# One late weight tile loaded in nine transfers: 96 partitions, then four times twelve tiny partitions and eight

## The chip, the cores and the metric

The kernel runs on one core of one Trainium2 chip. The metric is device time of one execution in microseconds (us). Three runs of the kernel before took 431.78, 432.27 and 433.0 us, so the median is 432.27 us.

## The reference

Two stages, in float32. First a linear attention with 8 batches, 8 heads, 576 positions and head size 64; then a spectral mixing of its output `x` (8 x 576 x 512) with 64 modes, each with a real and an imaginary 512 x 512 weight matrix.

```python
def phi(x):
    proj = np.einsum('bhsd,df->bhsf', x, w_phi)
    proj = proj - np.max(np.abs(proj), axis=-1, keepdims=True)
    return np.concatenate([np.exp(proj), np.exp(-proj)], axis=-1)
q_p, k_p = phi(q), phi(k)
num = np.einsum('bhsf,bhfd->bhsd', q_p, np.einsum('bhsf,bhsd->bhfd', k_p, v))
den = np.einsum('bhsf,bhf->bhs', q_p, np.sum(k_p, axis=2))[..., None] + 1e-06
x = num / den                                   # then heads side by side: (8, 576, 512)
X = np.fft.rfft(x, axis=1); Xr, Xi = real and imaginary part of X[:, :64]
Yr = einsum('bmd,mde->bme', Xr, w_r) - einsum('bmd,mde->bme', Xi, w_i)
Yi = einsum('bmd,mde->bme', Xr, w_i) + einsum('bmd,mde->bme', Xi, w_r)
u = x + np.fft.irfft(Y, n=576, axis=1)          # Y is zero above mode 63
out = u + np.maximum(u @ w_ch, 0.0)
```

The weights `w_r` and `w_i` are 64 x 512 x 512 float32 each, 134 MB together. They are the bulk of what the kernel reads.

## The kernel before

**Weights.** The 512 input channels are cut into four groups `g` of 128, the 64 modes into eight octets `o`. A weight tile `wt`, named by `(g, w)` with `w = 2*o + i` (`i` 0 for `w_r`, 1 for `w_i`), holds eight modes and 128 channels as bfloat16: 128 partitions with four rows of 1024 elements each, 1 MB in on-chip memory, 2 MB of float32 in HBM. There are 64 such tiles. `wload(g, w)` issues the one load of a tile from GpSimd (POOL), which converts on the way. A row of 1024 elements is the unit that one DMA engine moves as one packet; a tile has 512 rows, which is 32 for each of the 16 DMA engines.

**Order of the loads.** The queue `wq` lists all tiles in the order in which they are wanted; `next_w(1)` takes the next. Nearly every matmul step `mix` that has used up a tile calls it, since it frees a buffer (pool `pw`, nine buffers). In the attention part (16 units, up to about 285 us) loads of `q`, `k`, `v` stand between the weights. In the last part (the loop `while mixq`) there are 24 mixes: first the tiles `(3, 0)` to `(3, 11)`, then the twelve late ones

`(1,12) (1,13) (2,12) (2,13) (3,12) (3,13) (1,14) (1,15) (2,14) (2,15) (3,14) (3,15)`

Between two mixes TensorE does parts of the output work (`fill`: `hold`, `Channels.product`, `Absorb.all`). Behind the last mix stands what needs the last octet: `yst`, `zst`, the copies to `yl`, the sums of the list `plan` and the stores to `out`.

**In order.** Every engine's instructions run in the order in which the program writes them (class `InOrder`, line 37, which is also the line that the profile shows for nearly everything). POOL issues all the loads of `q`, `k`, `v` (but a few, which SyncE issues) and the weights, one behind the other.

**Completion semaphores.** The framework gives the transfers that POOL issues eight completion semaphores in turn. Each landing adds 16 to its semaphore, one for each of the 16 DMA engines. Before a transfer is issued, POOL waits until the transfer that had the same semaphore, eight transfers earlier, has landed, and then for its buffer. So at most eight transfers of POOL are under way at any time, of whatever size.

**A transfer of v in parts.** The last unit's `v` is loaded by SyncE in transfers of 57, 64 and 7 partitions (`load_v_parts`), issued at 248.17 us.

Of the kernel before, what the change touches and what calls it, by code (L numbers as in the profile page):

```python
# [11 lines left out]
BF16 = mybir.dt.bfloat16  # L12
# [10 lines left out]
MG = 8  # L23
# [20 lines left out]
def kernel(  # L44
# [15 lines left out]
    pool, sp = InOrder(tc, nc.gpsimd), InOrder(tc, nc.sync)  # L60
# [274 lines left out]
    def home(g, w):  # L335

        if g == 0 and w in (0, 9):
            h = w // 9
            t = yacc.bitcast(BF16).rearrange("p o e -> p (o e)")[:, 4096 * h:4096 * h + 4096]
        elif g == 0 and w == 5:  # L340
            t = XTb[1].rearrange("p u r t x b m -> p (u r t x b m)")
        elif g == 0 and w in (3, 12, 13):
            t = xs[:, max(w - 10, 1)].rearrange("p b n d -> p (b n d)")[:, 0:4096]
        else:
            return pw.tile([128, 4, 2, DMODEL], BF16, name="wt", tag="wt")
        return t.rearrange("p (m r e) -> p m r e", m=4, r=2)

    def wload(g, w):
        wt = home(g, w)
        o, i = w // 2, w % 2  # L350
        w = (moe_w_r, moe_w_i)[i]
        pool.dma_start(
            wt.rearrange("p m r e -> p m (r e)"),
            w[MG * o:MG * o + MG, g * 128:(g + 1) * 128, :].rearrange(
                "m (p r) e -> p m (r e)", r=2))
        return wt

    wts = {}
    wq = [(g, mg) for g in range(NG) for mg in range(12 if g else 2 * NO)]
# [6 lines left out]
    def next_w(n):  # L366
        for _ in range(n):
            if wq:
                key = wq.pop(0)
                wts[key] = wload(*key)  # L370
# [68 lines left out]
    for t in range(3):  # L439
        r = slice(32 * t, 32 * t + 32)  # L440
        dve.tensor_scalar_mul(out=minus[r], in0=ident_f[r, r], scalar1=-1.0)
    every = mf[0:96, 0:32]
    for t in range(3):
        r = slice(32 * t, 32 * t + 32)
# [167 lines left out]
    pb = pb_cm.__enter__()  # L612
# [340 lines left out]
    while mixq:  # L953
        key = mixq.pop(0)
        g, o, i = key[0], key[1] // 2, key[1] % 2
# [16 lines left out]
        if left > 12:  # L972
            n = -(-max(len(todo) - A - 3, 0) // (left - 12))
        elif left == 12:
            n = len(todo) - A
        else:
            n = math.ceil(len(todo) / max(left - 2, 1)) if left else 0
# [93 lines left out]
```

## Time and profile before

| | |
|---|---|
| runs, us | 431.78, 432.27, 433.0 |
| the profiled execution, us | 432.76 |
| its span, first to last instruction, us | 430.9 |
| PE, DVE, ACT, POOL busy share of the span | 75%, 70%, 69%, 28% |
| traffic of the DMA engines | 97.71 MB as written, 227 GB/s mean |
| HBM read and written | 163.64 MB and 9.44 MB |
| DMA engines' busy share, 307 to 341 us | 1.12 (over 1: packets overlap on an engine) |

The profiled execution is 1.86 us longer than its span. All times below count from the span's start. The profile's `MB` of a load counts what is written, half of what is read for a weight tile. "To landing" is the time from the start of the POOL instruction that issues a transfer to the last of the 16 increments of its semaphore.

### The profile page before, as it was taken

How to read it: one execution, taken by the hardware profiler on the slowest of the kernel's cores; microseconds unless marked ns; L12 is line 12 of the kernel's file. 1: busy time of each engine (PE TensorE's matmuls, PEld its weight loads, DVE VectorE, ACT ScalarE, POOL GpSimd, SP SyncE). 2: the span in 40 equal slices, each digit the busy share in tenths (PEclk: the TensorE clock that was granted, in tenths of full speed). 3: DMA queues.
4: the chain of work that ended last, by engine and by line, in shares of the span. 5: the costliest groups of instructions: out<-in, count | busy, mean ns of one | idle time of the engine just before them, and what ended most of it. 6: DMA issues, size and time to landing. Idle time of an engine off the chain costs nothing.

```text
span 430.9 us, 10044 instructions
## 1 busy us (share of the span) xinstructions
PE 324.9 (75%) x4162; PEld 195.6 (45%) x4207; DVE 302.7 (70%) x596; ACT 299.1 (69%) x487; POOL 122.2 (28%) x160
## 2 busy tenths in 40 slices
PE   1677577678787776876877767967899789886992
PEld 1345455446464553654645545543455333322320
DVE  6758767766677767878877878868645656882794
ACT  3787886877879779888878779765644345652772
POOL 6232132022321212322222321221022025750880
PEclk9979898889988989998988989899899999998998
DMA  9999999999999999999999999999999999997797
GB/s 211 210 211 211 238 213 237 224 225 238 240 210 233 216 237 238 238 211 239 212 239 222 226 244 229 212 212 212 212 212 213 212 211 212 212 212 161 244 395 288
DMA packets 49880, 97.71 MB, mean 227 GB/s; under 512 B 2315, under 2 KB 11531, under 8 KB 49835
## 3 DMA queue, kind: packets, MB, share of 16 engines
q0 software_dynamic: 45136, 85.40, 101.3%
q1 hardware_dynamic: 4538, 11.60, 7.2%
q8 instruction: 33, 0.54, 0.5%
q10 hardware_dynamic: 160, 0.07, 0.1%
q14 instruction: 13, 0.10, 0.1%
HBM read 163.64 MB, written 9.44 MB: 402 GB/s over the span
## 4 chain that ended last, share of the span: by engine, by line
PE 34%; ACT 24%; DMA 20%; DVE 14%; issue 4%; POOL 2%; ACTq 0%; POOLq 0%; DVEq 0%
DMA wt<-in_moe_w_i_dram 14%; PE pt L37 13%; PE one L37 11%; ACT AQ L37 10%; ACT AB L37 7%; PE two L37 6%; DMA kb<-in_k_dram 6%; DVE m L37 5%; PE pp L37 3%; ACT qT L37 3%; ACT XT L37 2%; DVE xs L37 2%; DVE xw L37 2%; DVE of L37 1%; DVE mk L37 1%
## 5 line engine op out<-in xcount | busy, mean ns | idle before, releaser
L37 ACT ACTIVATE AQ<-two 128x1024 bf16<-128x1024 f32 x64 | 80.6, 1348 | 2.1 <-PE two L37 2.0
L37 ACT ACTIVATE AB<-two 128x1024 bf16<-128x1024 f32 x64 | 62.8, 1055 | 3.3 <-DVE mk L37 3.0
L37 DVE TENSOR_REDUCE m<-two 128x8 f32<-128x1024 f32 x32 | 39.1, 1223 | 22.2 <-PE two L37 22.0
L37 ACT CAST xw<-pt 128x512 bf16<-128x512 f32 x54 | 31.8, 588 | 26.9 <-PE pt L37 26.7
L37 DVE TENSOR_REDUCE mk<-two 128x8 f32<-128x1024 f32 x32 | 38.9, 1219 | 9.2 <-PE two L37 9.2
L37 PE MATMUL pt<-wchb,xT 128*128 128x512 bf16 x135 | 37.0, 387 | 8.9 <-DVE xT L37 2.4
L37 POOL DMA_DIRECT2D wt<-in_moe_w_i_dram x28 | 21.1, 753 | 77.2 <-PE pt L37 37.2
L37 PE MATMUL two<-w2blk,qT 128*128 128x256 bf16 x128 | 23.9, 319 | 24.1 <-ACT AQ L37 13.6
L37 DVE TENSOR_TENSOR va<-vn,ee 128x1152 bf16<-128x1152 f32 x32 | 42.0, 1355 | 0.0
L37 POOL DMA_DIRECT2D wt<-in_moe_w_r_dram x30 | 22.5, 749 | 55.4 <-PE one L37 27.7
L37 PEld LDWEIGHTS <-xs 128*128 128x128 bf16 x624 | 31.1, 102 | 12.7 <-issue 5.9
L37 ACT COPY qT<-one 128x512 bf16<-128x512 bf16 (+1 forms) x32 | 19.0, 642 | 23.0 <-PE one L37 22.9
L37 PEld LDWEIGHTS <-qT 128*128 128x128 bf16 x144 | 15.3, 108 | 39.0 <-issue 35.0
L37 PE MATMUL two<-mT,minus 96*128 96x512 bf16 x64 | 26.5, 414 | 3.0 <-issue 0.9
L37 POOL DMA_DIRECT2D kb<-in_k_dram x16 | 11.4, 714 | 59.4 <-PE one L37 52.5
L37 DVE TENSOR_TENSOR xs<-one,rd 128x384 bf16<-128x384 f32 x48 | 26.8, 557 | 1.6
L37 PE MATMUL one<-kvz,AQ 128*128 128x65 bf16 x512 | 25.9, 203 | 0.9 <-ACT qT L37 0.8
L37 PEld LDWEIGHTS <-XT 128*32 128x32 bf16 x512 | 14.4, 149 | 27.0 <-issue 17.2
L37 PEld LDWEIGHTS <-AQ 128*128 128x128 bf16 x512 | 23.2, 104 | 7.1 <-issue 3.0
L37 PE MATMUL one<-wt,XT 128*32 128x512 bf16 x272 | 23.8, 438 | 3.4 <-ACT XT L37 3.4
L37 PE MATMUL two<-w2blk,kT 128*128 128x256 bf16 x128 | 21.1, 293 | 5.1 <-ACT AB L37 5.1
L37 PE MATMUL one<-CF,xs 128*128 128x64 bf16 (+2 forms) x480 | 23.2, 204 | 1.8 <-DVE xs L37 1.2
(151 smaller groups left out, 722.4 us busy)
## 6 DMA issues: line engine op xcount, KB each, us to landing
wt<-in_moe_w_r_dram POOLq DMA_DIRECT2D x30, 1024.0 KB, 26.3
wt<-in_moe_w_i_dram POOLq DMA_DIRECT2D x28, 1024.0 KB, 27.4
out_dram<-of SPq DMA_DIRECT2D x15, 512.0 KB, 3.4
vn<-in_v_dram POOLq DMA_DIRECT2D x13, 576.0 KB, 24.9
kb<-in_k_dram POOLq DMA_DIRECT2D x16, 288.0 KB, 19.6
qb<-in_q_dram POOLq DMA_DIRECT2D x16, 288.0 KB, 18.7
xs<-in_moe_w_i_dram POOLq DMA_DIRECT2D x2, 1024.0 KB, 23.3
out_dram<-of SPq DMA_DIRECT2D x6, 256.0 KB, 3.0
```

The source lines that it names most:

```text
L37: ins = f(*args, **kwargs)
```

## The change

`wload` is left as it was for 63 of the 64 tiles. The load of tile `(1, 12)`, written `(g, o, i) == (1, 6, 0)`, the first of the twelve late ones, becomes nine transfers. The first has partitions 0 to 95. Then follow four pairs: a load of 8 columns of the first 12 rows of `w_phi` into a new tile `few`, which nothing reads, and a load of eight partitions of the weight tile. All nine are issued by POOL, where the one was issued.

```diff
-        pool.dma_start(
-            wt.rearrange("p m r e -> p m (r e)"),
-            w[MG * o:MG * o + MG, g * 128:(g + 1) * 128, :].rearrange(
-                "m (p r) e -> p m (r e)", r=2))
+        dst = wt.rearrange("p m r e -> p m (r e)")
+        src = w[MG * o:MG * o + MG, g * 128:(g + 1) * 128, :].rearrange(
+            "m (p r) e -> p m (r e)", r=2)
+        if (g, o, i) != PIECES:
+            pool.dma_start(dst, src)
+            return wt
+        few = pb.tile([12, 32], BF16, name="few", bufs=1)
+        pool.dma_start(dst[0:96], src[0:48])
+        for n in range(4):
+            pool.dma_start(few[:, 8 * n:8 * n + 8], w_phi[0:12, 8 * n:8 * n + 8])
+            pool.dma_start(dst[96 + 8 * n:104 + 8 * n], src[48 + 4 * n:52 + 4 * n])
         return wt
+
+    PIECES = (1, 6, 0)
```

The order on PE, DVE, ACT and SP is the same in the built programs. On POOL there are eight transfers more, and the names of the semaphores that they wait for are these (SW0 to SW7 for the eight; `PE` is the wait for the buffer):

```
wt (3,11)                  128x4x1024   waits SW1, PE
wt (1,12), 96 partitions    96x4x1024   waits SW2, PE
few                              12x8   waits SW3, and writers and readers that lie before 290 us
wt (1,12), partitions 96..    8x4x1024  waits SW4
few                              12x8   waits SW5
wt (1,12), partitions 104..   8x4x1024  waits SW6
few                              12x8   waits SW7
wt (1,12), partitions 112..   8x4x1024  waits SW0
few                              12x8   waits SW1
wt (1,12), partitions 120..   8x4x1024  waits SW2
wt (1,13)                  128x4x1024   waits SW3, PE
```

Nine transfers in place of one shift the turn of the eight semaphores by a whole round, so every transfer behind them keeps the semaphore that it had.

## The prediction

> **What bounds the kernel now.** I read the page first, for the resource that is never idle.
>
> ```profile
> span 430.9 us, 10044 instructions
> DMA  9999999999999999999999999999999999997797
> q0 software_dynamic: 45136, 85.40, 101.3%
> ```
>
> The DMA engines are busy in every slice but the last four, and the queue that POOL's transfers use takes all of their time. The chain of waits shows where that reaches the end of the kernel, and the waits of PE whether anything softens it.
>
> ```profile
> 369.25 26.36 DMA wt<-in_moe_w_i_dram
> 395.65 0.84 PE pt L37 x8
> PE pt L37 <- DMA wt<-in_moe_w_i_dram: 2.4, 1, 2.4
> PE pt L37 <- DMA wt<-in_moe_w_r_dram: 0.9, 1, 0.9
> ```
>
> The load of tile (3,15), issued at 369.25, lands at 395.6; PE starts its eight matmuls 0.04 us later, having stood idle for 2.4 us, and 0.9 us before tile (3,14). Everything behind 395.65 hangs on this landing. So a shift of the last landing moves the end by as much, and a delay of the tiles before it costs nothing while it stays under their slack (below).
>
> Next the issue of the loads on POOL, with what each waited for, and the landings.
>
> ```profile
> 275.68 0.74 POOL L37 DMA_DIRECT2D wt<-in_moe_w_r_dram  x1 [3.13 <-PE one L37]
> 278.78 0.74 POOL L37 DMA_DIRECT2D wt<-in_moe_w_i_dram  x1 [2.35 <-PE one L37]
> 281.82 0.74 POOL L37 DMA_DIRECT2D wt<-in_moe_w_r_dram  x1 [2.30 <-PE one L37]
> ...
> 288.94 0.74 POOL L37 DMA_DIRECT2D wt<-in_moe_w_i_dram  x1
> 291.69 0.74 POOL L37 DMA_DIRECT2D wt<-in_moe_w_r_dram  x1 [2.01 <-PE pt L37]
> 299.84 0.74 POOL L37 DMA_DIRECT2D wt<-in_moe_w_i_dram  x1 [7.41 <-PE pt L37]
> 307.62 0.74 POOL L37 DMA_DIRECT2D wt<-in_moe_w_r_dram  x1 [7.03 <-PE pt L37]
> 313.06 0.74 POOL L37 DMA_DIRECT2D wt<-in_moe_w_i_dram  x1 [4.71 <-PE pt L37]
> ```
>
> The changed load is the one at 307.62; the answers for the single loads give 33.4 us to its landing, so 341.0. The six before it, (3,6) to (3,11), land by the same reading at 311.3, 316.3, 321.2, 326.1, 331.1 and 336.1, and (1,13) at 346.0. One tile lands every 4.95 us (4.96 from (1,13) to (3,15)): 0.155 us for each of an engine's 32 rows. The queue is some 34 us deep, which is six to seven tiles, each on a semaphore of its own, of eight.
>
> ```profile
> POOL wchb L37 <- DMA wt<-in_moe_w_r_dram: 3.9, 1, 3.9
> ```
>
> This line, of POOL's waits, shows that the eight semaphores do hold POOL up: `wchb` shares no buffer with a weight tile, yet its load waited 3.9 us until the transfer eight places before it had landed (issued at 117.46, landed at 146.6; `wchb` went out at 146.91).
>
> Last the sixteen increments of each landing, in the trace's records. Those of (1,12) run from 335.9 to 341.0: four engines at 335.9 to 336.6, one at 338.2, eleven at 339.6 to 341.0. This spread of 5.1 us is the same for every tile from 300 us on: four engines are ahead by some 4 us, and a tile is there when the slowest is.
>
> **The change, part by part.** *Rows taken off.* With 96 partitions an engine gets 24 rows for 32: 8 x 0.155 = 1.24 us less, so the large part lands at 341.0 - 1.2 = 339.8. Alone that would be a gain of 1.2 us, as the queue ends with its slowest engine.
>
> *Eight more transfers on POOL.* By the rows nearest in size (0.53 us for a `yl` of 16 partitions) they cost 8 x 0.53 = 4.2 us of POOL's time. Alone that is free: POOL idles 15.3 us before the issue at 348.60, and its first sum comes at 351.40.
>
> *Waits.* Here lies the price. The nine transfers take nine turns of eight semaphores, of which six or seven are held by tiles still in the queue. So POOL issues: 96 partitions at 307.6; first tiny load at 308.4; first eight partitions when (3,6) has landed, 311.3; then one transfer for each landing, at 316.3, 321.2, 326.1, 331.1 and 336.1. The fourth piece has the semaphore of the 96 partitions themselves, so it waits for 339.8, by which time all but a few rows of what was queued has been moved. Behind it on POOL, in order, stand (1,13), (2,12), (2,13), (3,12), (3,13) and (1,14), which went out from 313.06 to 332.57 and now go out from 340.4 on, 0.74 us apart. For PE the first of them is wanted at 352.68. The DMA engines run dry, and this is time of the resource that sets the end.
>
> *Restart.* What is lost is the time from an issue into an empty queue to data. Before 398 us the trace has no empty queue; the nearest row is the last `yl`, which POOL issues at 400.86 and which lands after 3.6 us.
>
> ```profile
> L37 POOL DMA_DIRECT2D yl<-zst x1: 532/532/532, 400.9 to 400.9; - x1
> ...
> DMA to landing us min/median/max: 3.6/3.6/3.6
> ```
>
> Its 128 KB take 0.6 us at the 212 GB/s of this stage, so the fixed part is 3.0 us. The far rows: SyncE's stores of 512 KB land in 3.4 us, 1.3 us of it data at 395 GB/s, so 2.1; the first `w_phi` load, 32 KB at the start of the program, takes 5.0. I take 3.0, the same engine, queue and state, and keep 2.1 and 5.0. The Trainium skill, page "DMA: Bandwidth & Descriptors", section "Anatomy of one DMA — SWDGE (gpsimd) path", gives a fixed cost of about 2.0 us; by it the sum below would be +2.1 us, and the trace's row is longer.
>
> *How many engines share a piece.* No POOL transfer in this trace uses fewer than 16. SyncE's loads of `v` do: of the 57 partitions three increments come late, together at 261.4 (57 is 3 x 19), of the seven partitions seven. So a transfer goes to a number of engines that divides it. Eight partitions from four source rows give eight engines or four, 0.62 or 1.24 us each; bounds are 16 engines (0.3) and one (4.95). I take four.
>
> *The sum.* The engines of the fourth piece: issue 339.85 + 3.0 + 1.24 + 4.95 = 349.0 for (1,13). The other twelve: 340.4 + 3.0 + 4.95 = 348.4. Before: 346.0. So (1,13) is 3.1 us late, the following tiles too, since from there on the queue is full again ((1,15) is issued at 348.60 as before, five tiles still queued), and (3,15) lands at 398.7. PE's slack between landing and use is 6.7 us for (1,13), 5.0 for (3,13), 4.5 for (2,14), 3.6 for (2,15): all above 3.1, so PE notices at (3,14) only, and the shift passes whole to the tail. The profiled execution took 432.76, so 435.9. It lay 0.5 above the median of its runs; from the median, 432.27 + 3.1 = **435.4**.
>
> **The rivals.** *A. The pieces fall on late engines.* Then pieces one to three, 3.7 us, follow 339.8 on them and cover the restart; the fourth and (1,13) follow at once: 339.8 + 3.7 + 1.24 + 4.95 = 349.7, +3.7, so 436.0. For it: eleven of sixteen engines are late, and the profile doesn't name the four that lead. On the leading four the three pieces are done by 338.4, before the restart, as in my sum. The page named above, section "Why a DMA increments its semaphore by 16 and not by 1", says that a POOL transfer on k engines takes k consecutive ones from a cursor that goes round; by that rule twelve and four bring the cursor back, and all four pieces fall on the same four. No run here shows it yet.
>
> *B. Balance without a stall (faster).* If the issues do not wait as I read it, the queue never empties: twelve engines save 1.24 us, the four leaders, 4.4 to 5.1 us ahead, carry 3.7 more and stay within it. The last landing comes 1.2 us earlier, 431.0; perfect balance (the mean of the sixteen increments is 339.2, against 341.0) would give 1.8. It decides if the fourth piece and (1,13) are issued by about 337, or the fixed part is under 0.6 us for the twelve engines. Against it: the wait of `wchb`, and the named semaphores.
>
> *C. A short restart (no change).* An empty queue may answer faster than 3.0 us. At 1.2 us the loss is down to 1.3 us. The shortest row, 2.1, speaks against it.
>
> *D. A piece is put on one engine.* The fourth then takes 4.95 on it: 339.85 + 3.0 + 4.95 + 4.95 = 352.8, +6.8, 439.1. The seven partitions on seven engines speak against it.
>
> **How the numbers follow.** My forecast gets 0.58, A 0.20, B 0.07, C 0.10, D 0.05. With the fixed part at 2.1 the forecast is +2.2 (434.5), at 5.0 it is +5.1 (437.4). The range, 433.2 to 437.2, holds the forecast nearly whole, A, and part of C; B, D and the ends are left out. A measurement can tell this kernel from no change from about 0.3%, 1.3 us, on. Faster by more: half of B, 0.03. Within: the rest of B, C, and a little of the forecast, 0.15. Slower: 0.82.
>
> **What would show it.** On POOL, between 307 and 342 us, tiny and eight-partition loads one for each landing, near 311, 316, 321, 326, 331, 336 and 340, and then six weight loads 0.74 us apart. In the windows a DMA share that falls near 340 to 343, and sixteen increments of (1,13) within about 1 us where they spread over 5. PE waits some 3 us longer for tile (3,14), and the last mix starts near 398.7. The prediction is wrong if POOL issues (1,13) before 335, or if the last mix starts before 396.9.

## The result, and the profile after

The changed kernel takes 436.95 us in the median of four runs (436.15 to 437.66), the kernel before 432.02 us in four (431.53 to 433.0): 4.9 us slower. The ratio on record is 1.0109, with an interval of 1.0092 to 1.0126 (it is not the quotient of the two medians, which is 1.0114). The profiled execution took 437.27 us, 4.5 more than that of before (432.76).

The page of the changed kernel:

```profile
span 435.4 us, 10101 instructions
DMA  9999999999999999999999999999999899998697
q0 software_dynamic: 45712, 85.40, 100.7%
```

The traffic is what it was; there is one slice more, the 32nd, in which the DMA engines were not busy throughout. The issues on POOL show why (start, duration, and in brackets the idle time before with what ended it):

```profile
306.65 0.68 POOL L37 DMA_DIRECT2D wt<-in_moe_w_r_dram  x1 [7.08 <-PE pt L37]
307.35 0.53 POOL L37 DMA_DIRECT2D few<-in_w_phi_dram  x1
311.57 0.63 POOL L37 DMA_DIRECT2D wt<-in_moe_w_r_dram  x1 [3.69 <-DMA wt<-in_moe_w_r_dram]
316.54 0.53 POOL L37 DMA_DIRECT2D few<-in_w_phi_dram  x1 [4.34 <-DMA wt<-in_moe_w_i_dram]
321.47 0.65 POOL L37 DMA_DIRECT2D wt<-in_moe_w_r_dram  x1 [4.40 <-DMA wt<-in_moe_w_r_dram]
326.41 0.53 POOL L37 DMA_DIRECT2D few<-in_w_phi_dram  x1 [4.29 <-DMA wt<-in_moe_w_i_dram]
331.37 0.63 POOL L37 DMA_DIRECT2D wt<-in_moe_w_r_dram  x1 [4.44 <-DMA wt<-in_moe_w_r_dram]
336.72 0.53 POOL L37 DMA_DIRECT2D few<-in_w_phi_dram  x1 [4.71 <-DMA wt<-in_moe_w_i_dram]
340.05 0.65 POOL L37 DMA_DIRECT2D wt<-in_moe_w_r_dram  x1 [2.81 <-DMA few<-in_w_phi_dram]
340.69 0.77 POOL L37 DMA_DIRECT2D wt<-in_moe_w_i_dram  x1
```

One transfer for each landing, 4.9 us apart; the fourth piece at 340.05, then (1,13), which before went out at 313.06. The DMA engines meanwhile, in 40 slices of 0.175 us from 338 to 345 us:

```profile
DMA  8666665564333110001180169969699999999999
```

They run out engine by engine, stand all but still near 341, and are full again from 343 on. From there the queue never empties, and the chain and PE's waits show the same end as before, only later (the chain: start, duration; the waits: total, times, longest):

```profile
368.25 31.87 DMA wt<-in_moe_w_i_dram
400.16 0.69 PE pt L37 x8
PE pt L37 <- DMA wt<-in_moe_w_r_dram: 4.7, 2, 4.3
PE pt L37 <- DMA wt<-in_moe_w_i_dram: 2.1, 2, 1.2
```

Tile (3,15) lands at 400.1 where it landed at 395.6: 4.5 us, the whole difference of the two profiled executions. From that landing to the last instruction both take 35.2 to 35.3 us.

### The profile page after: what moved, and what is told of

The parts are those of the page before. It is cut to its first block, busy times and chain, and to the rows that moved or that the text cites. A ratio compares the mean times of both kernels' runs of the same rounds, so it can differ in the third digit from the quotient of the medians.

```text
span 435.4 us, 10101 instructions
## 1 busy us (share of the span) xinstructions
PE 329.1 (76%) x4207; PEld 195.0 (45%) x4207; DVE 302.7 (70%) x596; ACT 298.9 (69%) x487; POOL 126.5 (29%) x168
## 4 chain that ended last, share of the span: by engine, by line
PE 34%; ACT 27%; DMA 19%; DVE 13%; issue 4%; POOL 1%; DVEq 0%; ACTq 0%; POOLq 0%
PE one L37 14%; ACT AQ L37 12%; DMA wt<-in_moe_w_r_dram 11%; PE two L37 9%; ACT AB L37 8%; PE pt L37 7%; DMA wt<-in_moe_w_i_dram 7%; DVE m L37 6%; PE pp L37 3%; ACT qT L37 3%; ACT XT L37 3%; DVE xs L37 2%; DVE mk L37 1%; DVE yacc L37 1%; POOL xw L37 1%
## 5 line engine op out<-in xcount | busy, mean ns | idle before, releaser
L37 PE MATMUL pt<-wchb,xT 128*128 128x512 bf16 x144 | 38.0, 387 | 8.4 <-DVE xT L37 2.4
L37 POOL DMA_DIRECT2D wt<-in_moe_w_r_dram x34 | 24.9, 733 | 66.0 <-PE one L37 34.3
L37 PE MATMUL two<-w2blk,qT 128*128 128x256 bf16 x128 | 22.8, 308 | 25.9 <-ACT AQ L37 13.7
L37 PE MATMUL two<-qT,w2blk 128*128 128x512 bf16 x64 | 26.9, 421 | 9.5 <-ACT AQ L37 9.5
```

The costliest lines, as they stand in the source:

```text
L37: ins = f(*args, **kwargs)
```

## The experiments

Two numbers are used below for each: when POOL issues (1,13), and when (3,15) lands, both from the profiled execution. The time from that landing to the last instruction is 32.8 to 35.3 us in the ten profiles, and why it varies is not shown. So the time of one profiled execution can be up to 2.5 us off what its landing says, and a few tenths between two medians are not read.

**Five transfers, without the tiny loads.**

```diff
-        few = pb.tile([12, 32], BF16, name="few", bufs=1)
         pool.dma_start(dst[0:96], src[0:48])
         for n in range(4):
-            pool.dma_start(few[:, 8 * n:8 * n + 8], w_phi[0:12, 8 * n:8 * n + 8])
             pool.dma_start(dst[96 + 8 * n:104 + 8 * n], src[48 + 4 * n:52 + 4 * n])
```

> The tile in 96 partitions and four of eight, without the four tiny loads: five transfers in place of one. Theory (the turn of the eight semaphores holds POOL until the queue is dry): five turns reach only as far as the load before the 96 partitions; POOL issues (1,13) near 326, (2,12) near 331, (2,13) near 336, all before the 96 partitions land at 339.8, the queue never empties, and the time is that of the kernel before within 0.7 us (ratio 0.998 to 1.002). Rival (small transfers of a few partitions, or their uneven place on the engines, cost the time): the same four pieces are there, so at least 3 us slower, ratio 1.007 or more.

Measured: 432.58 us, ratio 1.0011 (0.9999 to 1.0022). POOL, and the same slices from 338 to 345 us:

```profile
326.90 0.78 POOL L37 DMA_DIRECT2D wt<-in_moe_w_i_dram  x1 [4.60 <-PE pt L37]
331.86 0.76 POOL L37 DMA_DIRECT2D wt<-in_moe_w_r_dram  x1 [4.18 <-DMA wt<-in_moe_w_r_dram]
...
DMA  9999999999999999999999999999999999999999
```

(1,13) goes out at 326.9, nothing runs dry, (3,15) lands at 396.2. The same four pieces of eight partitions cost next to nothing, so the pieces by themselves are not what costs.

**Nine transfers, without the pieces.**

```diff
-        few = pb.tile([12, 32], BF16, name="few", bufs=1)
-        pool.dma_start(dst[0:96], src[0:48])
-        for n in range(4):
+        few = pb.tile([12, 64], BF16, name="few", bufs=1)
+        pool.dma_start(dst, src)
+        for n in range(8):
             pool.dma_start(few[:, 8 * n:8 * n + 8], w_phi[0:12, 8 * n:8 * n + 8])
-            pool.dma_start(dst[96 + 8 * n:104 + 8 * n], src[48 + 4 * n:52 + 4 * n])
```

> The tile in one load as before, and behind it eight tiny loads of 12 partitions that nothing reads: nine transfers, but no piece of the tile. Theory: the ninth has the semaphore of the tile's own load and waits for it, near 341.0; POOL issues (1,13) near 341.6, 1.2 us later than in the changed kernel, but no engine carries a fourth piece; the last mix starts near 399.5 to 401, time 436 to 437.5, ratio 1.009 to 1.012. Rival (the pieces cost it): eight tiny loads are eight times 0.53 us on a POOL that idles, ratio within 1.002 of 1.

Measured: 437.56 us, ratio 1.0117 (1.0099 to 1.0136); (3,15) lands at 400.7. The end of POOL's series:

```profile
336.37 0.50 POOL L37 DMA_DIRECT2D few<-in_w_phi_dram  x1 [4.47 <-DMA wt<-in_moe_w_i_dram]
341.31 0.50 POOL L37 DMA_DIRECT2D few<-in_w_phi_dram  x1 [4.44 <-DMA few<-in_w_phi_dram]
341.83 0.78 POOL L37 DMA_DIRECT2D wt<-in_moe_w_i_dram  x1
```

A tile in one piece is as slow as the change when nine turns are taken. The eighth tiny load goes out at 341.31, where the tile's own last increment stands at 341.0 (the trace names the tiny load that landed 0.2 us after it).

**The tiny loads from SyncE.** `pool.dma_start(few...)` becomes `sp.dma_start(few...)`, with `few` in float32.

> The changed kernel with its four tiny loads issued by SyncE (into float32), the tile's five transfers by POOL as they are: the same nine transfers on the same sixteen DMA engines, but five turns of POOL's semaphores for nine. Theory (POOL's turns): POOL issues (1,13) near 327 and the time is that of the kernel before, ratio 0.998 to 1.002. Rival (tiny transfers disturb the queue): as slow as the changed kernel, ratio 1.009 or more.

Measured: 433.02 us, ratio 1.0019 (1.0006 to 1.0033). (1,13) goes out at 327.1 and (3,15) lands at 396.2. The waits on POOL in this kernel are those of five transfers, and of the change's 1.09% some 0.2% is left.

```profile
291.03 1.53 SPq L37 DMA_DIRECT2D few<-in_w_phi_dram  x4
327.12 0.78 POOL L37 DMA_DIRECT2D wt<-in_moe_w_i_dram  x1 [4.59 <-PE pt L37]
```

The first line shows a limit of this test: SyncE issues the four tiny loads at 291.0, 19 us before the 96 partitions (310.3), so they no longer lie between the pieces. That tiny loads at their old place in the queue disturb it is not excluded here; what they cost there is read from the two kernels with seven transfers.

**Seven transfers: two tiny loads.** `few` is loaded for `n < 2` only.

> 96 partitions, tiny, eight, tiny, eight, eight, eight: seven transfers. Theory: POOL issues (1,13) when (3,11) has landed, near 336.1, and (2,12) when the 96 partitions have, near 340. The leading engines idle for 1 to 2 us, the late ones have the rest of their rows until 339.8 and are fed in time: 0 to 0.7 us slower, ratio 1.000 to 1.002. A loss in proportion to the number of transfers (the rival, a price for each small transfer) would give six eighths of the change's 4.9 us: 3.7 us, ratio 1.0085.

Measured: 433.39 us, ratio 1.0036 (1.0021 to 1.0051); (3,15) lands at 397.6.

```profile
337.20 0.78 POOL L37 DMA_DIRECT2D wt<-in_moe_w_i_dram  x1 [4.66 <-DMA wt<-in_moe_w_i_dram]
```

It is above what I gave (1.000 to 1.002), and far below a price in proportion (1.0085). Between seven turns and nine the loss trebles: at seven the next tile is issued while the late engines still have rows, at nine it is not. Of the 2.0 us by which (3,15) lands later, 0.6 stand at (3,11) already, which lies ahead of the tile, 0.3 more at (1,13), and 1.1 come in the last step, from (3,14) to (3,15) (6.09 us for 5.00; below).

**Seven transfers: the whole tile and six tiny loads.** As the kernel with eight, with `range(6)`. It was to explain the part above the expectation.

> The tile in one load as before, and six tiny loads of 12 partitions behind it: seven turns, of which the last waits for (3,11), so POOL issues (1,13) near 336.4, before the tile's own landing near 341, and the queue does not empty. Theory (a transfer costs every one of the sixteen engines its place in the ring, 0.17 to 0.2 us, also where it has no data there, as the increments of the tiny loads in the earlier runs stand that far apart): 6 x 0.18 = 1.1 us slower, the last landing 1.1 us later, ratio 1.0015 to 1.004. Rival (only the turns of the semaphores cost): ratio 0.999 to 1.001.

Measured: 434.90 us, ratio 1.0063 (1.0043 to 1.0083); (1,13) at 336.9, (3,15) lands at 397.2, 1.6 us later than before. The place that each tiny load takes is there: the last increment of (1,12) stands at 341.24, that of the sixth tiny load at 342.29, in steps of 0.17 to 0.19 us. But the tile behind them does not land 1.05 us later: (1,13) lands at 346.6 where it landed at 345.95, and 0.2 us of these 0.6 stand at (3,11) already. Most of the rest, 0.95 us, comes in the last step, from (3,14) to (3,15): 5.95 us for 5.00. So the price of six tiny loads is some 0.4 us at the next landing, well under mine. Nor did the queue stay full on all engines: seven increments of (1,13) come at 344.1 to 344.5, 7.3 to 7.6 us after its issue, as at a restart. Why the median of its runs (433.1 to 435.4) lies above the profiled 434.07, and the interval above mine, is open.

**Eight more tiny loads, behind the fourth piece.**

```diff
-        few = pb.tile([12, 32], BF16, name="few", bufs=1)
+        few = pb.tile([12, 96], BF16, name="few", bufs=1)
...
             pool.dma_start(dst[96 + 8 * n:104 + 8 * n], src[48 + 4 * n:52 + 4 * n])
+        for n in range(4, 12):
+            pool.dma_start(few[:, 8 * n:8 * n + 8], w_phi[0:12, 8 * n:8 * n + 8])
```

> The changed kernel with eight more tiny loads behind the fourth piece. Theory (once the queue is dry, every us of POOL is a us at the end): their semaphores are free by then, each costs POOL 0.53 us, so (1,13) is issued near 345.0 in place of 340.7, the last landing comes near 404.4, time 441.2, ratio 1.020 to 1.022. Rival (POOL's issue time stays hidden, the loss is a fixed restart): the same time as the changed kernel, ratio 1.009 to 1.012.

Measured: 439.87 us, ratio 1.0183 (1.0159 to 1.0208).

```profile
340.68 4.10 POOL L37 DMA_DIRECT2D few<-in_w_phi_dram  x8
344.77 0.80 POOL L37 DMA_DIRECT2D wt<-in_moe_w_i_dram  x1
```

The 4.1 us that POOL spends on them move the issue of (1,13) by 4.1 us, its first increment by 4.2 (347.9 to 352.1) and the last landing to 404.0, by 3.8. With a full queue POOL's issue time was hidden; with an empty one it is paid one to one, or nearly. The median moved less than the landing, by 2.9 us, and the ratio is below the 1.020 that I gave as the least; the rival, a fixed loss, is further off.

**Instruction fetches moved.** The trace of the changed kernel has a 16 KB instruction fetch in the DMA queues at 343.10, 1.59 us long, in the middle of the restart:

```profile
q8 instruction: 1, 0.02, 1.0%
```

(that is the window 340 to 350 us: 1.0% of sixteen engines' 10 us). To move it, 64 transposes were put on PE early:

```diff
+        if n == 2:
+            spin = one([128, 128], BF16)
+            for _ in range(64):
+                pe.transpose(spin, ident_b, ident_b)
```

> The changed kernel with 64 more transposes on PE early in the attention part (their result is not read). They bring PE's instruction fetches, 16 KB each and in the changed kernel at 328.65, 343.10 and 367.85, about half a distance forward, to about 320, 336 and 355, away from the restart near 341. Theory (one engine is 0.9 us behind all others at the landing of (1,13) because the fetch at 343.10 went through it): no engine is that late, (1,13) lands by about 348.9 in place of 349.7, and the last landing comes 0.3 to 1 us earlier than in the changed kernel; ratio 1.008 to 1.011. Rival (the late engine is late for another reason): the last increment of (1,13) stays 0.8 us or more behind the fifteenth, 7.3 us or more behind the issue of (1,13) by POOL plus 1.5.

Measured: 436.27 us, ratio 1.0101 (1.0074 to 1.0128). The fetches stand at 337.25 and 359.09. In each kernel's trace, the times to landing of the two transfers issued at 340.0 to 340.8 or 340.7 (minimum, median, maximum; the maximum is (1,13)), the changed kernel first:

```profile
DMA to landing us min/median/max: 3.8/6.4/9.0
```

```profile
DMA to landing us min/median/max: 4.0/6.2/8.3
```

From an issue at 340.69 and 340.71 the tile is there at 349.7 and at 349.0. In the changed kernel fifteen increments of it come from 347.9 to 348.85 and the last at 349.67; with the fetch moved all sixteen come from 348.0 to 349.05. (3,15) lands at 399.5, 0.6 us earlier. The times alone would not tell the two kernels apart, so this is shown for one profiled execution of each.

**A better balance tried in another place.** The kernel before, with the last `v` in two parts:

```diff
-            for p0, p1 in ((0, 57), (57, 121), (121, 128)):
+            for p0, p1 in ((0, 119), (119, 128)):
```

> The kernel before, with the last unit's v loaded by SyncE in parts of 119 and 9 partitions in place of 57, 64 and 7: 119 is 7 x 17, so seven engines should take 17 partitions each, nine take one each, and seven engines none of v. Theory (the slowest engine ends the queue, four to five of the lowest engines are ahead by 4 us): the late engines lose three or four partitions of 4.6 KB, 0.17 us each, so the spread of the sixteen increments after 300 us falls from 5.1 to about 4 or less and the last landing comes 0.5 to 0.7 us earlier: 431.4, ratio 0.998 to 0.999. Rival (the sum of all rows counts, not the slowest engine): no difference that can be told, ratio 1.000.

Measured: 435.27 us, ratio 1.0075 (1.0059 to 1.0091). The expectation failed in direction. Seven engines did take the large part (seven increments of it at 261.5 to 262.4), but the spread of a tile's increments grew from 5.1 to 8.3 us, and (3,15) landed at 397.8. So at least one of these seven was among the late ones. What stands is that the slowest engine counts: the last landing moved by 2.2 us although not a byte more was loaded.

## Why the prediction was right, step by step

**The waits.** Right, to the instruction: the series of issues is the predicted one (307.6, 308.4, 311.3, 316.3, 321.2, 326.1, 331.1, 336.1, 339.8, then 340.4) within 0.7 us; only the first two came 1.0 us earlier, as this execution reached them earlier. The sign that was to refute it, (1,13) issued before 335, did not come: it went out at 340.69. Taking the tiny loads off POOL, by leaving them out or by issuing them from SyncE, removes nearly all of the loss; keeping nine turns without the pieces keeps it.

**The restart.** The term was too large. From the issue of (1,13) to its first increment are 7.2 us in the changed kernel, of which 4.95 are rows: 2.3 us, and 2.2 to 2.35 in the three other kernels that ran dry. I took 3.0 from the `yl` row. (The upper bound, 5.0, is the median of two loads of `w_phi`; the first of them took 4.3. Neither bound was reached.) By the trace the Trainium skill's figure (page "DMA: Bandwidth & Descriptors", section "Anatomy of one DMA — SWDGE (gpsimd) path", about 2.0 us) was the nearer of the two.

**How many engines share a piece.** Right, four: of the fourth piece twelve increments come at 341.6 to 342.1 and four at 343.7 to 343.9. On these (1,13) is 0.7 us behind the rest, as in the sum (349.0 against 348.4).

**Where the pieces fall.** Rival A, three pieces one behind the other on the same late engines, is refuted, and so is the reading that put all four on the same engines; but the first piece did fall on late engines, as A's name says. (The prediction has the three pieces done on all four leaders by 338.4; by its own rows that is the first of the four, and the last is done by 339.1, which changes nothing in the sum.) An engine without data passes a transfer about 0.19 us after the one before. Taking that step from the first tiny load's increments gives those of the first piece but for four engines: 337.01 to 338.03, 338.50 to 339.49, 339.24 to 340.34 and 339.96 to 341.06, the slowest engine and three others, none of the leading four. In the second piece two of the leaders have data, 334.97 to 336.07 and 335.15 to 336.34. The kernel without tiny loads shows the same groups. So the pieces go round by fours with or without the tiny loads. This agrees with the Trainium skill's cursor for the pieces (same page, section "Why a DMA increments its semaphore by 16 and not by 1") but not with twelve engines for a load of twelve partitions: that load left the cursor where it was. The section names an exception, direct copies that count as sixteen engines although some have no data, which would fit; no run here shows that it is the reason.

**The other rivals.** B needed (1,13) issued by about 337; it went out at 340.69 and the queue had emptied. Its balance fails too: the first piece goes wholly to late engines and the second by half, so the four leaders do not carry the 3.7 us that would have balanced them. The five-transfer kernel, which never stalls, is no faster than before. C needed a restart of about 1.2 us, and it took 2.2 to 2.35. D needed one engine for the fourth piece, and there were four.

**What the sum left out.** The predicted shift was 3.1 us, the measured one 4.5 in the profiles and 4.9 in the medians. Fifteen engines brought (1,13) by 348.85, 2.9 us after the 345.95 of before: the restart was 0.7 us shorter than in the sum, the issues were 0.2 to 0.3 us later. On top come two terms of 0.8 us each that I did not have. That the first and the restart nearly cancel is luck.

First, one engine brought (1,13) at 349.7, 0.8 us behind the others; the fetch at 343.10 fits it, and with the fetches moved no engine was behind.

Second, from (1,13) to (3,15) it took 50.4 us where it took 49.7 before. A part, 0.2 us, is left of a fetch: with the one at 367.85 the last engine fell back by 0.4 us and made up half of it in the next tile. In the trace of before, the fetches of this stretch (345.67, 370.04 and 394.34) did not delay the last increment: the engines were up to 5.1 us apart, and the last increments kept their steps of 4.93 to 5.06 us. The larger part, 0.6 us, is the last step, from (3,14) to (3,15): 5.62 us for 5.00. A fetch lies in it too, at 398.10, but it is not what makes it long. In the kernel with the fetches moved, none lies between 381.42 and 409.81, yet its (3,15) lands 5.52 us after (3,14), its whole stretch takes 50.4 us too, and PE's mixes of the two tiles stand as far apart:

```profile
394.02 1.08 PE L37 MATMUL pt<-wt,XT 128*32 128x512 bf16 x8 [3.21 <-DMA wt<-in_moe_w_r_dram]
399.54 0.66 PE L37 MATMUL pt<-wt,XT 128*32 128x512 bf16 x8 [1.31 <-DMA wt<-in_moe_w_i_dram]
```

The ten traces fall into two groups. Where all or some engines ran dry, the sixteen increments of (3,15) lie within 1.9 to 3.1 us and the last step takes 5.5 to 6.1 us. Where none did, they lie 5.2 us or more apart, and it takes 4.7 to 5.0. Behind (3,15) POOL's queue holds only the `yl` loads, in packets of 4 KB; in the 2.5 us before the landing these take 315 to 380 ns each in the first group and 174 to 252 in the second. That they hold up the last tile when all engines reach them at once would fit; it was not tried.

**PE's slack.** I let PE notice at (3,14). It waits already for (3,13), (2,14) and (2,15), whose mixes start 0.04 us after their landings, since the landings came later than the sum said and PE had come to this part 1.0 us earlier. It changes nothing: the last two tiles decide.

## What to carry to other kernels

Where transfers share a fixed number of completion semaphores, the depth of a queue is counted in transfers, not in bytes. A tiny transfer put ahead of a large one takes the turn of a megabyte, and a split of one load is to be costed by the landing that its last part, and the load behind it, will wait for. Here the loss was 0.1% with five transfers and 0.4 to 0.6% with seven, where the next load was issued before the late engines ran out. With nine and more the queue was empty, and the restart was paid, with nearly all the time of the instructions that the issuer still had ahead of the load: 1.1 to 1.8%.

## What the runs showed of the hardware that I had not expected

- A transfer takes its place on all sixteen engines, also where it has no data: 0.17 to 0.2 us on each between the increments of two tiny loads in a full queue. Six such places moved the next tile's landing by 0.4 us only.
- The increments' spread is a cushion. In the kernel before, instruction fetches of 16 KB (0.9 to 1.0 us each) left the steps between the last increments at 4.9 to 5.1 us, with the engines 5.1 us apart; in the changed kernel, with the engines within 2 us, the one at 343.10 (1.59 us) came with a last increment 0.8 us behind the rest, the one at 367.85 with 0.4.
- Twelve partitions in one POOL load did not move the place at which the next short transfer starts; eight partitions from four source rows moved it by four engines.
